# The setup and the first batch of a DFT and bilinear layer kernel in another order: folds as rows arrive, a third table buffer, weight conversion spread over three units

## The chip, the cores and the metric

One core of a Trainium2 chip runs the whole program. TensorE (PE) multiplies, VectorE (DVE), ScalarE (ACT) and GpSimd (POOL) do element work, SyncE (SP) starts most transfers; ACT and POOL start some too. The metric is the device time of one execution in microseconds (us); the median of several runs stands for a kernel.

## The reference

```python
def _attn_ref(x):                      # x: 8 x 3072 x 256, f32
    X = np.fft.fft(x, axis=1)
    X = np.fft.fft(X, axis=2)
    return X.real.astype(np.float32)

def _moe_ref(x, w_a, w_b, w_out):      # 256 x 1536, 256 x 1536, 1536 x 256
    a = x @ w_a
    b = x @ w_b
    return (a * b @ w_out).astype(np.float32)
```

The real part of a two-dimensional DFT over sequence and features is followed by a bilinear layer: two products with weights, multiplied element by element, and a third product. The weights come as 64-bit values and are turned into 32-bit floats on the chip.

## The kernel before

The work is split into high and low halves of each f32 number (`gh` and `gl`, `XH[0]` and `XH[1]`, `W[:, 0]` and `W[:, 1]`), and three products of halves make one f32 product (`PASSES`). The feature DFT is put into the weights: a **weight chunk** (`WChunk`, six of them) multiplies a converted piece of `w_a` or `w_b` by a cosine or sine table `wt` and writes a high and a low half of `W`, and its first row to `w128` by way of DRAM. `Conv` turns a raw 64-bit piece into f32 halves in seven steps: two on ACT ("p", L324 and L325), three on DVE ("a", L326 to L328), the high half on ACT ("b", L329) and the low half on DVE or POOL ("c", L330).

Along the sequence, symmetry folds four row sets to one: `fold_ops` makes for each of three row pairs sums and differences into `F` in twelve operations (numbered 0 to 11 in the code), the even ones on one engine, the odd ones on another. For batch 0 both are DVE; for later batches they are POOL and DVE. `FN` holds the middle column. `xh_split` splits `F` into `XH`, and the chunks **P**, **N0** (or **NA**) and **Q** (`DftP`, `DftN0`, `DftNA`, `DftQ`, 18 matmuls of some 384 columns each) multiply it by tables `tab` that POOL loads into two rotating buffers. Their results are `PQ` (cosine and sine part, two halves each) and `PN` (the Nyquist column). `half` 0 and 1 give the two halves of the sequence.

The loop has 36 **units** per batch, for three column groups `st` and twelve feature tiles `ft`. Unit u does the even matmuls (`mm_e`, L549, six of 512 columns) and the Nyquist term (L553, DVE, which needs `w128`); the down products of the unit before last (`mm_d`, L625, 24 of 256 columns); the odd matmuls (`mm_o`, L564), and for the unit before `post1` (L573 on DVE, a copy `bc` on ACT) and `post2` (the product `g` of L583 on DVE, the mirrored one of L588 on POOL in the first 17 units of batch 0 and on DVE later, the high casts L584 and L589 on ACT, the low halves L592 on POOL). A PSUM pair `ab` is free again after L583. There are two such pairs and four tiles `d`.

Nothing is reordered by a scheduler: the order of the program is the order on each engine (`manual_schedule`). Batch 0 has no batch before it, so its folds, its DFT and the first weight conversions are done in a setup, written out line by line, in a pool `set_p` whose memory `PQ` and `PN` take later. The other conversions, the DFT of `half` 1 and the folds of batch 1 are hung between the units of batch 0 as hooks:

```python
    FOLDS0 = ("raw", (0, 1, 2, 3, 4, 5), (6, 7, 8, 9, 10, 11))
...
    FIRST = {
        0: [DftP(0, 1)],
        1: [DftN0(1)],
        2: [DftQ(0, 1)],
        4: [(conv_in, "a1")],
        5: [(conv_out, "a1")],
...
        13: [(conv_out, "b2"), (nyq.load,)],
        14: [wc[3]],
```

`conv_in` does steps "p" and "a" at one place, `conv_out` "b" and "c" a unit later. `nyq.load` starts 32 transfers of 768 single elements on SP, for the Nyquist columns of the later batches (`NyqTurn`). Partial sums of batch 0 go to DRAM (`part`) and come back.

Of the kernel before, what the change touches and what calls it, by code (L numbers as in the profile page):

```python
# [14 lines left out]
TW = 386  # L15

@with_exitstack
def fft2_real__then__bilinear_moe_kernel(
# [87 lines left out]
    def fold_ops(b, rp, raw, e0, e1, tmp=None):  # L106
# [4 lines left out]
        s1, s2, ms = ((FT if tmp is None else tmp)[:, k] for k in range(3))  # L111
# [163 lines left out]
    class DftQ:  # L275
# [3 lines left out]
        def mm(self):  # L279
# [10 lines left out]
        def post(self, lo_eng=nc.gpsimd):  # L290
            b, half, ps = self.b, self.half, self.ps
            cols, _, _ = halves(half)
            a = bc_p.tile([P, 512], F32, tag="bc", name="bc")
# [58 lines left out]
    class WChunk:  # L352
# [17 lines left out]
        def post(self):  # L370
# [8 lines left out]
            nc.sync.dma_start(w128[:, 4 * c : 4 * c + 4], row)

    def run(fs):
        for f in fs:
            f()
# [639 lines left out]
```

## Time and profile before

| | before |
|---|---|
| median of 3 runs | 1899.04 us (1896.61 to 1900.35) |
| the profiled execution, device time | 1900.28 us |
| its span in the trace | 1898.5 us |
| PE busy | 1790.8 us, 94% |
| DVE, POOL, ACT busy | 1364.7, 1090.4, 698.0 us |
| mean granted PE clock | 0.976 |

The span runs from the first to the last instruction in the trace; 1.8 us of the execution's time lie outside of it. Idle time of an engine counts only where the engine that ends last waits for it. A granted clock of 1.00 is 2.4 GHz and 0.50 is 1.2 GHz.

### The profile page before, as it was taken

The numbers are of one execution on the slowest core, as the hardware profiler recorded it, in microseconds if no ns is written. First come the engines' busy times: TensorE is split into PE (matmuls) and PEld (weight loads), VectorE is DVE, ScalarE is ACT, GpSimd is POOL, SyncE is SP. The second block draws the span as 40 slices with busy tenths as digits, with TensorE's granted clock in tenths as the row PEclk, the third lists the DMA queues.
The fourth block names the chain that finished last, engine by engine and source line by source line (L and its number), as shares of the span: only waits on it lengthen the run. The fifth ranks groups of instructions, "written<-read, shape, count | busy, mean of one in ns | idle before, by whom it ended". The sixth has DMA issues, their size and how long they took to land.

```text
span 1898.5 us, 29035 instructions
## 1 busy us (share of the span) xinstructions
PE 1790.8 (94%) x11146; PEld 1612.0 (85%) x11146; DVE 1364.7 (72%) x2056; ACT 698.0 (37%) x1239; POOL 1090.4 (57%) x887
## 2 busy tenths in 40 slices
PE   2777768999999999999999999999999999999998
PEld 2666657889899998999999989999899998999888
DVE  5556467677876787778776787678776887666766
ACT  2444312433344333333344333333344333333332
POOL 1355455666656665566656665576655666554343
PEclk8798888999999999999999999999999999999999
DMA  6322321332013210222013211222012310210030
GB/s 219 122 93 89 37 78 45 140 98 76 12 57 103 98 45 32 76 89 94 14 56 103 98 45 31 76 90 81 26 57 88 114 45 26 82 56 8 18 26 23
DMA packets 101259, 131.34 MB, mean 69 GB/s; under 512 B 55247, under 2 KB 79967, under 8 KB 94207
## 3 DMA queue, kind: packets, MB, share of 16 engines
q1 hardware_dynamic: 89662, 58.92, 11.0%
q0 software_dynamic: 10896, 70.03, 10.8%
q8 instruction: 87, 1.43, 0.3%
q10 hardware_dynamic: 560, 0.52, 0.1%
q14 instruction: 54, 0.43, 0.1%
HBM read 100.98 MB, written 28.46 MB: 68 GB/s over the span
## 4 chain that ended last, share of the span: by engine, by line
PE 83%; DVE 0%; POOL 0%; ACT 0%; issue 0%; ACTq 0%
PE d L625 39%; PE ab L564 19%; PE ab L549 19%; PE ab L175 5%; PE ab L698 0%; PE ab L694 0%; DVE F L128 0%; POOL gl L592 0%; PE ab L726 0%; PE ab L723 0%; DVE T L573 0%; ACT stg L636 0%; ACTq L528 0%; POOL RAW L118 0%; DVE T L553 0%
## 5 line engine op out<-in xcount | busy, mean ns | idle before, releaser
L592 POOL TENSOR_TENSOR gl<-g,gh 128x512 fp32r<-128x512 f32 x574 | 753.9, 1335 | 595.8 <-ACT gh L584 595.6
L625 PE MATMUL d<-WO,gh 128*128 128x256 f32 x4608 | 830.5, 281 | 0.0
L625 PEld LDWEIGHTS d<-WO,gh 128*128 128x128 f32 x4608 | 728.7, 189 | 26.1 <-ACT stg L636 0.3
L625 PE MATMUL d<-WO,gl 128*128 128x256 f32 x2304 | 647.3, 281 | 0.2
L573 DVE SCALAR_TENSOR_TENSOR T<-T,ab 128x512 f32<-128x512 f32 x576 | 391.5, 685 | 332.5 <-PE ab L564 328.3
L564 PE MATMUL ab<-PQ,W 128*128 128x512 f32 x1728 | 458.6, 401 | 44.1 <-DVE T L553 44.0
L549 PE MATMUL ab<-PQ,W 128*128 128x512 f32 x1728 | 457.6, 400 | 21.2 <-DVE g L583 16.7
L553 DVE SCALAR_TENSOR_TENSOR T<-PN,w,ab 128x512 f32<-128x512 f32 x576 | 412.9, 745 | 78.0 <-PE ab L549 54.6
L625 PEld LDWEIGHTS d<-WO,gl 128*128 128x128 f32 x2304 | 435.6, 189 | 1.5 <-POOL gl L592 1.3
L549 PEld LDWEIGHTS ab<-PQ,W 128*128 128x128 f32 x1728 | 329.3, 191 | 101.4 <-DVE g L583 18.0
L564 PEld LDWEIGHTS ab<-PQ,W 128*128 128x128 f32 x1728 | 307.0, 190 | 101.6 <-DVE T L553 47.5
L574 ACT COPY bc<-ab 128x512 f32<-128x512 f32 x288 | 169.4, 588 | 603.8 <-DVE T L573 603.8
L584 ACT CAST gh<-g 128x512 fp32r<-128x512 f32 x288 | 179.1, 622 | 419.4 <-DVE g L583 416.0
L583 DVE TENSOR_TENSOR g<-ab,bc 128x512 f32<-128x512 f32 x288 | 196.6, 683 | 33.6 <-ACT bc L574 28.9
L588 DVE TENSOR_TENSOR g<-T 128x512 f32<-128x512 f32 x271 | 205.3, 757 | 0.1
L589 ACT CAST gh<-g 128x512 fp32r<-128x512 f32 x288 | 178.7, 621 | 29.7 <-DVE g L588 18.2
L175 PE MATMUL ab<-tab,XH 128*128 128x384 f32 (+1 forms) x576 | 110.3, 346 | 23.9 <-DMA tab<-in_tabs_dram 23.9
L175 PEld LDWEIGHTS ab<-tab,XH 128*128 128x128 f32 x576 | 106.1, 196 | 26.8 <-issue 23.9
L88 POOL TENSOR_TENSOR PQ<-T,PQ 128x768 fp32r<-128x768 f32 x30 | 55.8, 1861 | 37.3 <-ACT PQ L87 29.8
L168 POOL DMA_DIRECT2D tab<-in_tabs_dram x48 | 26.9, 562 | 85.9 <-PE ab L175 85.9
L88 POOL TENSOR_TENSOR XH<-F,XH 128x768 fp32r<-128x768 f32 x30 | 55.7, 1869 | 5.7 <-ACT XH L87 5.7
L636 ACT COPY stg<-d 128x512 f32<-128x512 f32 x94 | 48.2, 596 | 9.2 <-PE d L625 8.1
(138 smaller groups left out, 677.7 us busy)
## 6 DMA issues: line engine op xcount, KB each, us to landing
tab<-in_tabs_dram POOLq DMA_DIRECT2D x48, 1158.0 KB, 5.5
RAW<-in_x_dram SPq DMA_DIRECT2D x44, 256.0 KB
out_dram<-stg SPq DMA_DIRECT2D x36, 256.0 KB
out_dram<-stg SPq DMA_DIRECT2D x12, 512.0 KB
PN<-nrow SPq DMA_DIRECT2D x14, 384.0 KB
out_dram<-stg SPq DMA_DIRECT2D x30, 128.0 KB
RAW<-in_moe_w_out_dram SPq DMA_DIRECT2D x3, 1024.0 KB
part<-stg SPq DMA_DIRECT2D x3, 1024.0 KB
```

The costliest lines, as they stand in the source:

```text
L175: nc.tensor.matmul(ps, lhs(lh, kt), tab[:, kt, rh, 0:n], start=(k == 0), stop=(k == 8))
L549: nc.tensor.matmul(ab[i], W[:, lh, 0, c : c + P], PQ[:, rh, st * 512 : (st + 1) * 512], start=(k == 0), stop=(k == 2), skip_group_check=True,)
L553: nc.vector.scalar_tensor_tensor(t[:, i, :], PN[:, st * 512 : (st + 1) * 512], w128[:, i * NFT + ft : i * NFT + ft + 1], ab[i], ALU.mult, ...
L564: nc.tensor.matmul(ab[i], W[:, lh, 1, c : c + P], PQ[:, 2 + rh, st * 512 : (st + 1) * 512], start=False, stop=(k == 2), skip_group_check=True,
L573: nc.vector.scalar_tensor_tensor(t[:, i, :], t[:, i, :], 2.0, ab[i], ALU.mult, ALU.subtract)
L574: nc.scalar.copy(bc, ab[1])
L583: nc.vector.tensor_tensor(g[:, 0, :], ab[0], bc, ALU.mult)
L584: nc.scalar.copy(gh[:, 0, :], g[:, 0, :])
L588: (nc.gpsimd if v["early"] else nc.vector).tensor_tensor(g[:, 1, ::-1], t[:, 0, :], t[:, 1, :], ALU.mult)
L589: nc.scalar.copy(gh[:, 1, :], g[:, 1, :])
L592: eng.tensor_tensor(gl[:, s, :], g[:, s, :], f32(gh[:, s, :]), ALU.subtract)
L625: nc.tensor.matmul(d[:, s, :], (gh, gl)[lh][:, s, q * P : (q + 1) * P], WO[:, rh, ft, :], start=(ft == first and s == 0 and k == 0), stop= ...
```

## The change

The setup: the row of zeros and its product are made first; each pair of rows is folded wholly when it has come, sums and differences, with the second pair's sums in a conversion's buffers; the middle column `FN` goes from DVE to POOL. A third table buffer `tab2` in the setup's pool holds the table of Q. P, N0 and the second weight chunk write to the `d` tiles of PSUM, so P, N0, Q and the first chunk follow each other. The `post` of each chunk is cut into pieces (`copy`, `sums`, `low`, `high`) that are placed one by one. Weight loads start on ACT's queue, the raw pieces lie in `STG` and `RAWW`, and the last of the setup's conversions is moved into units 0 and 1.

Batch 0: a conversion is spread over three units, its first ACT step a unit ahead of the second and of DVE's; ACT's steps stand between the two high casts of `post2` (`slot`), DVE's behind L583 (now L637). Two of the raw pieces use the table buffers. The 32 gathers are started four per unit over eight units. The folds of batch 1 take three or four operations per unit in units 15 to 26 instead of six in every third unit, and in all later batches the differences go into the buffers of the sums. The Nyquist turn moves from unit 18 to 24.

```diff
@@ fold_ops
-        md1, md2 = xb[:, :, 0:P], xc[:, :, 0:P]
+        md1, md2 = (v[:, :, 0:P] for v in ((xb, xc) if b == 0 else (s1, s2)))
...
-                nc.vector.tensor_tensor(FN[:, q, r2], s1[:, :, P], s2[:, :, P], op)
+                nc.gpsimd.tensor_tensor(FN[:, q, r2], s1[:, :, P], s2[:, :, P], op)
@@ the setup
-        wraw = as_raw(set_p.tile([P, 2048], F32, name="wraw"))
-        FT1 = set_p.tile([P, 3, 2, D], F32, name="FT1")
+        tab2 = set_p.tile([P, 3, 2, TW], F32R, name="tab2")
...
-        cva, cvb, cvo = Conv(wraw, *ca), Conv(STG, *cb), Conv(RAWW, us[0], wo_dst(0))
+        cva, cvb, cvo = Conv(STG, *ca), Conv(RAWW, *cb), Conv(STG, us[0], wo_dst(0))
...
+        rows_zero()
...
-        fold(0, (0, 1, 4, 5))
+        fold(0, (0, 2, 1, 3, 4, 5, 6, 7))
         fold(1, (0, 1, 4, 5))
-        fold(0, (8, 10))
+        wload(STG, wa_src(0), 2, nc.scalar)
+        fold(0, (8, 10, 9, 11))
+        fold(1, (2, 3, 6, 7))
         fold(2, (0, 1, 4, 5))
+        wload(RAWW, wa_src(3), 2, nc.scalar)
+        nc.gpsimd.dma_start(wt.rearrange("p a b c d -> p (a b c d)"), wtab)
+        nc.gpsimd.dma_start(tab2.rearrange("p a b c -> p (a b c)"), tabs[2])
+        tabq[(0, 2)] = tab2
         fold(1, (8, 10))
         fold(2, (8, 10))
+        nc.scalar.copy(XH[:, 0, 0], F[:, 0])
+        fold(1, (9, 11))
+        fold(2, (2, 3))
         fn_split(0)
+        V.tensor_tensor(XH[:, 1, 0], F[:, 0], f32(XH[:, 0, 0]), ALU.subtract)
+        p0.mm(d_tiles(0, 2))
+        n0.mm(d_tiles(1, 3))
+        cva.do("p", V)
+        fold(2, (6, 7, 9, 11))
+        cva.do("a", V)
+        sign_ops(1)
...
+        q0.mm()
+        p0.copy()
+        fn_split(1)
+        cvb.do("p", V)
+        cva.do("c", V)
+        wa0.mm()
...
-    p0.post(V)
-    cva.do("c", V)
-    wa0.mm()
-    cvb.do("p", V)
-    n0.post()
-    q0.mm()
+    p0.sums()
+    n0.copy()
     cvb.do("a", V)
+    p0.extra()
+    q0.copy()
     cvb.do("b", V)
-    wload(STG, wa_src(1), 2)
+    wload(RAWW, wa_src(1), 2)
+    n0.sums()
     cvb.do("c", V)
-    wa0.post()
-    wb0.mm()
-    q0.post(V)
+    wb0.mm(d_tiles(0, 2))
+    wa0.high()
+    p0.low(V)
+    q0.sums()
+    wa0.low()
+    q0.split(V)
+    wb0.high()
     cvo.do("p", V)
+    wb0.low()
     sign_ops(3)
     xh_split(1, 0, nc.gpsimd)
     xh_split(1, 1, nc.gpsimd)
-    wb0.post()
-    cvo.do("a", V)
-    wload(RAWW, wa_src(4), 2)
-    cvo.do("b", V)
-    cvo.do("c", V)
@@ post2 and the units
             if v["early"]:
                 minus()
+                for f, *a in slot:
+                    f(*a)
                 lo(nc.gpsimd, 0)
...
+            minus_high()
             lo(nc.gpsimd, 1)
...
-    FOLDS0 = ("raw", (0, 1, 2, 3, 4, 5), (6, 7, 8, 9, 10, 11))
+    FOLDS0 = ((0, 1, 2), (3, 4, 5), (6, 7, "raw"), (8, 9, 10, 11))
...
+        0: [(cvo.do, "a", V), (cvo.do, "b", V), DftP(0, 1)],
+        1: [(cvo.do, "c", V), (conv_step, 0, "p"), DftN0(1)],
+        2: [DftQ(0, 1), (weights_later,), (conv_step, 0, "a")],
+        16: [(conv_step, 5, "c"), (fold_zero,), (load_part, 0)],
+        24: [(lambda: (nyq.mm(), nyq.post()),), (load_tab, 0, 0), (load_tab, 0, 1)],
...
+    for k in range(1, 6):
+        SLOT[2 * k + 2] = [(conv_step, k - 1, "b"), (conv_step, k, "p1")]
+        SLOT[2 * k + 3] = [(conv_step, k, "p2"), (conv_step, k, "a")]
+        FIRST[2 * k + 3] = [(conv_step, k - 1, "c")]
+    SLOT[15] = [(conv_step, 5, "b")]
+    for k in range(8):
+        FIRST.setdefault(14 + k, []).extend(([(nyq.load,)] if k == 0 else []) + [(nyq.load_rows, k)])
...
-                hook(fold_step, b + 1, i - 18 if b == 0 else i)
+                hook(fold_step, b + 1, i - 15 if b == 0 else i)
```

On ACT, at the end of the setup, before (`ab_189` and `ab_209` are the results of P and N0, `ab_281` that of the first chunk, `ab_302` that of Q):

```order
L214 ACTIVATE bc<-ab_189,zb 128x385
L87 CAST EX<-bc 128x1
L87 CAST PQ<-T 128x768
L324 ACTIVATE u<-stg 128x1024
L325 ACTIVATE s<-stg 128x1024
L240 ACTIVATE bc<-ab_209,zb 128x385
L243 COPY EXN<-bc 1x1
L329 CAST gh<-u 128x1024
L375 CAST W<-ab_281 128x512
```

and now (`d_206` and `d_226` are P and N0, `ab_261` is Q, `ab_292` the first chunk):

```order
L219 ACTIVATE bc<-d_206,zb 128x385
L87 CAST FNH<-FN 128x6
L365 ACTIVATE u<-RAW 128x1024
L366 ACTIVATE s<-RAW 128x1024
L225 CAST PQ<-T 128x768
L262 ACTIVATE bc<-d_226,zb 128x385
L87 CAST EX<-bc 128x1
L323 COPY bc<-ab_261 128x384
L325 COPY EXT<-ab_262 128x1
L370 CAST gh<-u 128x1024
L273 COPY EXN<-bc 1x1
L416 CAST W<-ab_292 128x512
```

The second conversion's two steps now stand ahead of the first cast to `PQ`, and the copies of N0 and Q behind it.

On ACT again, in the units of batch 0, around a conversion, before (`ab_693` and `ab_755` belong to two units that follow each other):

```order
L329 CAST XH<-F 128x1024
L574 COPY bc<-ab_693 128x512
L584 CAST gh<-g 128x512
L589 CAST gh<-g 128x512
L324 ACTIVATE F<-RAW 128x1024
L325 ACTIVATE F<-RAW 128x1024
L574 COPY bc<-ab_755 128x512
```

and now:

```order
L628 COPY bc<-ab_584 128x512
L638 CAST gh<-g 128x512
L370 CAST XH<-F 128x1024
L365 ACTIVATE F<-tabw 128x1024
L645 CAST gh<-g 128x512
L628 COPY bc<-ab_637 128x512
L638 CAST gh<-g 128x512
L366 ACTIVATE F<-tabw 128x1024
L645 CAST gh<-g 128x512
```

The two steps stood together behind both casts to `gh`; now each stands between the two casts of a unit, in two units.

On SP, late in batch 0, before (L379 stores and reads `w128`, L752 are the gathers, L95 row loads of batch 1):

```order
L639 DMA part_384<-stg 128x2048
L748 DMA nyx<-in_mirror_dram 128x128
L752 DMA nyx<-in_x_dram 128x6x1 x32
L379 DMA w_83<-FT 128x1x4
L95 DMA RAW<-in_x_dram 128x512 x2
```

and now:

```order
L807 DMA tabw<-in_mirror_dram 128x128
L813 DMA tabw<-in_x_dram 128x6x1 x4
L418 DMA w_83<-FT 128x1x4
L813 DMA tabw<-in_x_dram 128x6x1 x4
L708 DMA part<-part_374 128x2048
L813 DMA tabw<-in_x_dram 128x6x1 x8
L95 DMA RAW<-in_x_dram 128x512 x2
L813 DMA tabw<-in_x_dram 128x6x1 x12
```

Four gathers stand ahead of the last transfer to `w128` instead of 32; the others lie among the row loads and stores.

## Rows read from the trace of the kernel before

**Rows 1.** Stages: window, its length, then busy us (instructions) of each engine, granted clock.
```profile
0.00:23.87 23.87, 0.00 (x0) 0.00 (x0) 13.16 (x37) 3.58 (x10) 8.36 (x14) 1.00 0.94 343
23.87:79.07 55.20, 31.31 (x116) 26.99 (x117) 30.49 (x48) 23.50 (x36) 7.57 (x7) 0.72 0.34 122
79.07:236.00 156.93, 123.99 (x681) 107.99 (x681) 87.06 (x117) 63.76 (x96) 82.01 (x63) 0.88 0.30 75
236.00:324.00 88.00, 66.43 (x376) 57.28 (x375) 59.53 (x89) 18.89 (x37) 50.04 (x44) 0.88 0.20 66
324.00:1898.50 1574.50, 1569.02 (x9979) 1419.77 (x9977) 1174.46 (x1768) 588.33 (x1060) 942.42 (x760) 1.00 0.20 63
```

**Rows 2.** Waits of PE, 0 to 79.07 us: total, times, longest.
```profile
PE ab L175 <- DMA tab<-in_tabs_dram: 23.9, 1, 23.9
PE ab L364 <- ACT bc L214: 9.5, 1, 9.5
```

**Rows 3.** Waits of PE, 79.07 to 324 us.
```profile
PE ab L564 <- DVE T L553: 37.1, 9, 11.1
PE ab L549 <- DVE g L583: 16.7, 3, 6.8
```

**Rows 4.** Stages again: first of seven half-clock stretches after 79.07 us, their sum.
```profile
128.25:135.08 6.83, 4.85 (x16) 4.29 (x17) 3.78 (x6) 4.53 (x7) 4.58 (x4) 0.50 0.46 155
...
sum 58.03, PE 33.13 PEld 28.08 DVE 31.10 ACT 19.57 POOL 25.91; mean PE 4.73 PEld 4.01 DVE 4.44 ACT 2.80 POOL 3.70
```

**Rows 5.** Chain that ended last, in order of time: start, us, what.
```profile
325.43 1.39 PE ab L564 x6
...
331.04 1.41 PE ab L564 x6
```

**Rows 6.** Timeline (start, us, [idle before]) of first folds; then the stage they open.
```profile
7.98 0.69 DVE L135 TENSOR_TENSOR FT<-RAW 128x512 f32<-128x512 f32 x1 [7.06 <-DMA RAW<-in_x_dram,rix]
...
10.70 0.69 DVE L136 TENSOR_TENSOR FT<-RAW 128x512 f32<-128x512 f32 x1 [2.03 <-DMA RAW<-in_x_dram,rix]
...
7.98:22.77 14.79, 0.00 (x0) 0.00 (x0) 11.97 (x34) 2.29 (x9) 3.02 (x4) 1.00 1.05 407
```

**Rows 7.** Stage of the setup's ACT list; timeline of POOL behind it.
```profile
42.75:63.20 20.45, 12.87 (x45) 10.29 (x45) 11.76 (x17) 13.66 (x23) 1.74 (x3) 0.75 0.45 167
...
62.52 3.58 POOL L88 TENSOR_TENSOR XH<-F,XH 128x768 fp32r<-128x768 f32 x2 [5.69 <-ACT XH L87]
```

**Rows 8.** Timeline around one conversion in the loop.
```profile
121.81 2.54 POOL L592 TENSOR_TENSOR gl<-g,gh 128x512 fp32r<-128x512 f32 x2
...
123.58 1.31 DVE L326 TENSOR_SCALAR F<-F 128x1024 uint32<-128x1024 uint32 x1 [4.25 <-ACT F L324]
125.03 1.23 DVE L327 CUSTOM_DVE_ANT_0 F<-F 128x2048 uint16<-128x2048 uint16 x1
...
130.23 2.93 PE L549 MATMUL ab<-PQ,W 128*128 128x512 f32 x6 [6.79 <-DVE g L583]
```

**Rows 9.** Line L326 in the setup: ns least/median/most, first and last start.
```profile
L326 DVE TENSOR_SCALAR u<-u x2: 686/686/687, 38.6 to 48.7; 128x1024 uint32<-128x1024 uint32 x2
```

**Rows 10.** Groups of DVE, 325 to 337 us: busy us, mean ns.
```profile
L553 DVE SCALAR_TENSOR_TENSOR T<-PN,w,ab 128x512 f32<-128x512 f32 x4 | 2.8, 744 | 0.0
L573 DVE SCALAR_TENSOR_TENSOR T<-T,ab 128x512 f32<-128x512 f32 x4 | 2.6, 682 | 1.4 <-PE ab L564 1.4
...
L583 DVE TENSOR_TENSOR g<-ab,bc 128x512 f32<-128x512 f32 x2 | 1.4, 682 | 0.0
```

**Rows 11.** Timelines of SP's queue and of DVE behind it.
```profile
199.59 22.56 SPq L752 DMA_DIRECT2D nyx<-in_x_dram  x32
...
224.91 0.75 DVE L553 SCALAR_TENSOR_TENSOR T<-PN,w,ab 128x512 f32<-128x512 f32 x1 [11.86 <-DMA w<-FT]
```

**Rows 12.** Timeline of DVE: the Nyquist turn, a fold of batch 1.
```profile
240.41 0.25 DVE L764 TENSOR_TENSOR nyx<-nyx,ab 128x96 f32<-128x96 f32 x1 [2.44 <-PE ab L757]
...
250.24 1.65 DVE L138 TENSOR_TENSOR RAW<-RAW 128x512 f32<-128x512 f32 x1
```

More of the change, by code (lines that the diff above doesn't have):

```diff
@@ L110, in fold_ops @@
         xa, xb, xc, xd = (raw[:, k] for k in range(4))
-        s1, s2, ms = ((FT if tmp is None else tmp)[:, k] for k in range(3))
+        s1, s2, ms = tmp or [FT[:, k] for k in range(3)]
         rv = (slice(None), slice(None, None, -1), slice(None))
@@ L182, in ab_tiles, with d_tiles, dft_pair @@
         return [ps_ab.tile([P, 512], F32, tag=f"ab{i}", name=f"ab{i}") for i in range(2)]
-    def dft_pair(even, odd, half, q, n0):
-        ps = ab_tiles()
+    def d_tiles(*q):
+        return [ps_d.tile([P, 2, D], F32, tag=f"d{k}", name=f"d{k}").rearrange("p a b -> p (a b)") for k in q]
+    def dft_pair(even, odd, half, q, n0, ps=None):
+        ps = ps or ab_tiles()
         m = even(0, 0).shape[-1]
@@ L303, in post, with split @@
             nc.vector.tensor_tensor(t[:, J : J + n1], cv, av[:, ::-1], ALU.subtract)
-            nc.scalar.copy(t[0:1, 0 : 2 * J], PN[0:1, cols])
-            split(lo_eng, PQ[:, 2, cols], PQ[:, 3, cols], t[:, 0 : 2 * J])
+        def split(self, lo_eng=nc.gpsimd):
+            cols, _, _ = halves(self.half)
+            nc.scalar.copy(self.t[0:1, :], PN[0:1, cols])
+            split(lo_eng, PQ[:, 2, cols], PQ[:, 3, cols], self.t)
+        def post(self):
+            self.copy()
+            self.sums()
+            self.split()
     class Conv:
@@ L376, in post, with low @@
             nc.scalar.copy(row.rearrange("o (p f) -> o f p", f=4), ps[1][0:1, :].rearrange("o (f p) -> o f p", f=4))
+            nc.sync.dma_start(w128[:, 4 * c : 4 * c + 4], row)
+        def low(self):
+            c, ps = self.c, self.ps
+            cols = slice(c * 512, (c + 1) * 512)
             for eo in range(2):
                 nc.vector.tensor_tensor(W[:, 1, eo, cols], ps[eo], f32(W[:, 0, eo, cols]), ALU.subtract)
[L379 to L383, printed above, removed]
+        def post(self):
+            self.high()
+            self.low()
     def conv_tiles():
@@ L819, in conv_out, with weights_later @@
-    def conv_out(k):
-        cv[k][0].do("b", V)
-        cv[k][0].do("c", nc.gpsimd)
+    later = [(RAWW, None, us[0], cx)]
+    cv = [Conv(RAWW, us[0], cx)]
+    def weights_later():
+        t = [
+            as_raw(tb_p.tile([P, 3, 2, TW], F32R, tag="tab", name="tabw").rearrange("p a b c -> p (a b c)")[:, 0:2048])
+            for _ in range(2)
+        ]
+        later.extend([
+            (t[0], (wa_src(4), 2), us[1], wo_dst(2)),
+            (t[1], (wo_src(1), 4), us[0], wo_dst(1)),
+            (RAWW, (wa_src(2), 2), us[1], cx),
+            (t[0], (wa_src(5), 2), us[0], wo_dst(2)),
+            (t[1], (wo_src(2), 4), us[1], wo_dst(2)),
+        ])
+        cv.extend(Conv(raw, u, hl) for raw, _, u, hl in later[1:])
+        conv_load(1)
+        conv_load(2)
+        nyq.t = t[0].bitcast(F32).rearrange("p n w -> p (n w)")
@@ L823, in fft2_real__then__bilinear_moe_kernel, with conv_load, conv_step @@
+    def conv_load(k):
+        wload(later[k][0], *later[k][1])
+    def conv_step(k, part):
+        cv[k].do(part, nc.gpsimd)
+        if part == "a" and k < 3:
+            conv_load(k + 3)
     wc = [WChunk(1, wt, *cx), WChunk(4, wt, *wo_dst(2)), WChunk(2, wt, *cx), WChunk(5, wt, *wo_dst(2))]
     FIRST = {
-        0: [DftP(0, 1)],
-        1: [DftN0(1)],
-        2: [DftQ(0, 1)],
-        4: [(conv_in, "a1")],
-        5: [(conv_out, "a1")],
-        6: [(conv_in, "b1"), wc[0]],
-        7: [(conv_out, "b1")],
@@ L934, in fft2_real__then__bilinear_moe_kernel @@
                     late_post = None
+                if prev is None or not prev["early"]:
+                    for f, *a in u[5]:
+                        f(*a)
                 if len(pend) >= 2:
```

164 lines of the change are left out of this document (79 added, 85 removed).

## The prediction

> **What bounds the kernel now.** I read the stage table first [rows 1]. From 324 us on TensorE is busy 1569.02 of 1574.50 us at a granted clock of 1.00; nothing in this change can shorten that. All that is to be had lies in the first 324 us. There PE is busy 31.31 + 123.99 + 66.43 = 221.7 us, so it is idle 102.3 us, and its clock is 0.72, 0.88 and 0.88 in the three working stages. The waits of PE say what for. Up to 79.07 us it is the start (23.9 us, a table of the DFT) and the setup (9.5 us, an ACT copy ahead of the first weight matmul) [rows 2]. From there to 324 us it is DVE: 37.1 us for the Nyquist term of L553 (longest 11.1) and 16.7 us for the product of L583 that frees a PSUM pair [rows 3]. No DMA stands in those two rows, but one is behind the longest wait, as the SP queue below shows.
>
> The lost clock is a cost of the same waits. In seven stretches at 0.50 (1.2 of 2.4 GHz), 58.03 us long, PE was busy 33.13 us [rows 4]; at 2.4 GHz that work takes half, so 16.6 us were lost, 2.4 per stretch. Each opens in or right behind an idle time of PE: the one from 128.25 [rows 4] in the wait of 6.79 us that ends at 130.23 [rows 8]. So the 244.9 us from 79.07 to 324 hold 190.4 us of PE work, which is 190.4 - 16.6 = 173.8 at the full clock, 54.5 of idleness and 16.6 of clock.
>
> A unit that nothing holds up takes PE 331.04 - 325.43 = 5.61 us, 1.39 of it the six odd matmuls [rows 5]. In the stage from 79.07 to 236 us DVE is busy 87.06 and POOL 82.01 us [rows 1], PE 123.99, some 113 of it at full clock. So in the units with weight conversion no other engine is the bound on average; order and latency are. From 236 to 324 us DVE has 59.53 us and PE, at full clock, about 60: there DVE has no room.
>
> **The change part by part.** *The setup, until the second unit begins (79.07 before).* The differences of rows 1 and half of those of rows 2 now stand on DVE ahead of the low half of XH, and the six small FN sums leave it. DVE needed 11.97 us from its first fold at 7.98 to the end of that half [rows 6]; four more operations of 512 columns (0.69 each [rows 6]) and four of half that width, less the small sums, make about 3.5. The second pair of rows came at 10.70 [rows 6]; DVE does two operations before it needs them, which leaves a hole of about 1.5. So XH is whole at 7.98 + 11.97 + 3.5 + 1.5 = 24.9, where the table let PE begin at 23.87. The weight loads no longer compete with the table, but DVE is then the limit: no gain at the start, a loss of 1 at most. The gain comes behind it: with the zero rows, FNH and a table for Q all there, P, N0 and Q run without the 9.5 us stop. A 512-column matmul takes 1.39/6 = 0.232 us, one of 384 columns 0.174 by proportion, 18 of them 3.1; the first group at half clock 6.3: 24.9 + 6.3 + 3.1 + 3.1 = 37.4. The first weight chunk follows at once.
>
> The new wait: PQ lies in memory that the third table buffer had, so ACT's first PQ cast waits for Q to end, at 37.4, and 20 more ACT instructions stand behind it, up to the sign flips and the XH casts that the second P needs. Before, the same kind of list, 42.75 to 63.20, held 13.66 us of ACT work [rows 7]; it loses a bias copy and one two-step preparation and gains two W casts and a row copy, so I take 13.0. ACT ends at 50.4, POOL's low half (3.58/2 = 1.8 [rows 7]) at 52.2, and the second P, 18 matmuls at half clock, at 58.5; the first unit fits in beside the casts. **The second unit begins at 58.5 instead of 79.07: -20.6 us.** Bounds: -12 (rows late, ACT held by DVE) to -24.
>
> *Conversions in the loop.* Before, the two ACT steps stood behind both gh casts, and all three DVE steps waited for them, in front of L573. Around 125 us that reads: L326 at 123.58, L327 at 125.03, L328 after it, and PE waits until 130.23, 6.79 us [rows 8]. Now the first ACT step stands a unit earlier and DVE finds its input. In such a unit DVE does 2 x 0.682 + 2 x 0.744 + 0.682 = 3.53 us of L573, L553 and L583 [rows 10], then 0.69 [rows 9] + 1.23 [rows 8] + 1.23 for L328 of the same width, to 6.68, then the next L573 and L553, 2.85, to 9.53. PE comes to the odd matmuls that need these at 5.61 + 5.61 - 1.39 = 9.83; since each half of a PSUM pair is released by itself, another 0.7 is slack: 1.0 in all.
>
> But POOL runs now while DVE converts. L326 shows that price: 0.686 us in the setup [rows 9], 1.31 when it began under a POOL pair that ran from 121.81 to 124.35 [rows 8]; it ended 0.54 us after POOL did, so it stood still meanwhile. L327 and L328 always met an idle POOL, so their price under one is not shown. A POOL operation takes 1.27 us (2.54/2 [rows 8]) and there are three in a unit. Bounds: nothing, or three of them less the slack, 3.8 - 1.0 = 2.8 us for each of six conversions, 17 us. I take 1.3 us, nearly two of them, 8 us in all, since L326 met one each time that POOL was at work. The ACT steps that now stand ahead of the second gh cast are in it.
>
> The Trainium skill, SBUF — State Buffer, section "SBUF: two separate sides", says that GpSimd and a DVE operation with two SBUF inputs or in a two-port mode take one shared port pair by an exclusive lock, the loser standing still for the whole instruction. The trace agrees for L326 (1.31 us, above). By that rule L327 and L328 pay as L326 does; it speaks against a change that first puts them under POOL work, and the sum by it is the first rival below.
>
> *The SP queue.* 32 gathers of single elements took 22.56 us of SP, with the 2 KB of w128 behind them, for which DVE waited 11.86 us [rows 11]. Now four gathers (2.8 us) stand ahead of that store, and a unit lies between it and its reader: nothing is left of the 11.1 us of PE idleness. The other gathers share SP with the row loads of batch 1.
>
> *Folds of batch 1.* Three operations per unit in units 15 to 26, not six in every third. The differences go into the sum buffers, so RAW is free one step earlier and a load has two units (11.2 us) to land, not one. Rows 2 of batch 1 still stand behind six stores and four gathers; I leave 2 us there, and 3 us for DVE under POOL: L138 took 1.65 us at 250.24 [rows 12], where an operation of 512 columns alone takes 0.69 [rows 6]. Units 15 and 16 carry a POOL product, a conversion's low half and folds: 2 us. The Nyquist turn, now at unit 24, makes DVE wait 2.44 us [rows 12] as before, but in a unit with folds: 2.5 us. Units 1 to 3, with the end of the setup's conversions: 1 us.
>
> **Sum of the loop.** 173.8 + 8 + 5 + 2 + 2.5 + 1 = 192.3, and 2.4 for one stretch at half clock: 194.7 instead of 244.9, **-50.2 us**. From batch 1 on nothing: PE is full there [rows 1], and the new homes of the differences only lengthen the time that rows may take. Together 20.6 + 50.2 = 70.8. The profiled execution took 1900.28 us (span 1898.5 and 1.8 around it), 1.2 above the median of the three runs: 1900.3 - 70.8 = 1829.5, say **1830 us**.
>
> **The rivals.** *DVE under POOL becomes the bound.* Every DVE step of a conversion stands still for one POOL operation: 17 us instead of 8; two half-clock stretches more, 4.8; 5 more in the folds, where DVE has no room: 1830 + 9 + 4.8 + 5 = 1849. For it speaks the 1.65 us of L138; against it, that no row shows L327 under POOL. It is the rule of the Trainium skill named above, worked out from rows.
>
> *The setup gains half.* ACT's list waits for DVE at each step, and Q ends later because its table lands late: the second unit begins at 69, 1840 us. The ACT copy in rows 2 speaks for it; that the weight operands are ready ahead of PE speaks against it.
>
> *Nothing stands any more.* Conversions and folds hide wholly: 8 + 5 + 2 + 2.4 less, and 24 for the setup: 1809 to 1813.
>
> *Slower.* The gathers hold up batch 1: 28 of 32 now stand among loads that POOL and DVE need. If each of the three groups of rows waits for a whole former queue of 22.56 us and loses one stretch of clock, 75 us go again: 1905. It decides from 70.8/3 = 23.6 us per group on. Against it: at most eight gathers (5.6 us) stand between the row loads' turn and their issue, with two units of lead.
>
> **How the numbers follow.** Forecast 0.52, DVE under POOL 0.21, half the setup 0.13, nothing left 0.10, level or slower by the gathers 0.04. The range takes in the first three and the upper edge of the fourth: 1812 to 1851. A measurement here tells 0.2% (4 us) from no change; every case but the last is faster: 0.96, 0.02 within, 0.02 slower.
>
> **What will show it.** Right: PE without a wait between P and the first weight chunk; ACT's first PQ cast right after Q; the second unit near 58 us; DVE's wait for w128 gone; PE full from about 255 us. Wrong: the first P before 22 or after 27 us; the conversion's steps on DVE stretched to 2 us or more each; PE waits of 4 us at the folds; row loads that land after their fold's turn.

## The result, and the profile after

The changed kernel takes 1829.06 us (median of 4; the kernel before, beside it, 1899.69): a ratio of 0.9632, 95% interval 0.9616 to 0.9649. The forecast was 1830. Its profiled span is 1827.2 us, 71.3 less than before. One execution of e9 (3539.3 us) took about twice and one of e2 (9950.5 us) over five times as long as the others of the run, and the ratios below leave them out.

The stages, as in [rows 1]: window, length, busy us (instructions) of PE, PEld, DVE, ACT and POOL, granted clock. The second unit begins at 56.36; the last stage is as long as before's from 324 on, 1574.5 us, and holds the same PE work, so the stage ahead of it is the old 79.07 to 324.

```profile
0.00:21.88 21.88, 1.87 (x9) 1.81 (x9) 15.58 (x39) 3.47 (x9) 12.70 (x18) 1.00 0.87 322
21.88:56.36 34.48, 28.24 (x109) 23.29 (x109) 28.99 (x39) 22.00 (x35) 8.54 (x9) 0.90 0.54 197
56.36:252.70 196.34, 180.22 (x1060) 157.28 (x1061) 152.26 (x207) 83.82 (x138) 140.19 (x108) 0.97 0.35 95
252.70:1827.20 1574.50, 1568.94 (x9972) 1419.93 (x9970) 1184.66 (x1766) 586.74 (x1059) 942.15 (x760) 1.00 0.20 63
...
151.26:154.68 3.42, 3.42 (x17) 3.22 (x16) 2.36 (x4) 2.86 (x5) 3.42 (x4) 0.50 0.00 0
226.36:233.18 6.82, 5.55 (x13) 4.33 (x14) 4.91 (x11) 2.21 (x6) 3.27 (x5) 0.50 0.16 34
```

So the part up to the second unit is 79.07 - 56.36 = 22.7 us shorter (forecast 20.6), and the loop behind it 244.9 - 196.34 = 48.6 (forecast 50.2). In the loop two stretches at half clock are left of seven [rows 4]; they cost (3.42 + 5.55) / 2 = 4.5 us instead of 16.6.

PE's waits, as in [rows 2, 3]: 0 to 56.36, then 56.36 to 145, then 145 to 252.7. The 2.3 of the second unit's start is counted in the first and the second group.

```profile
PE d L176 <- DMA tab<-in_tabs_dram: 16.0, 1, 16.0
...
PE ab L603 <- DVE g L637: 2.3, 1, 2.3
PE ab L618 <- DVE T L607: 1.9, 1, 1.9
PE d L176 <- DVE XH L515: 0.8, 1, 0.8
...
PE ab L603 <- DVE g L637: 5.8, 4, 2.3
PE d L685 <- POOL gl L648: 2.4, 4, 0.8
PE ab L618 <- DVE T L607: 2.3, 2, 1.1
...
PE ab L618 <- DVE T L607: 4.6, 3, 3.4
PE ab L603 <- DVE g L637: 2.5, 1, 2.5
```

The stop of 9.5 us for L214 and the 11.1 us behind `w128` are gone, and behind the table's arrival no wait is longer than 3.4 us.

### The profile page after: what moved, and what is told of

It is laid out like the page before. It is cut to its first block, busy times and chain, and to the rows that moved or that the text cites. A ratio compares the mean times of both kernels' runs of the same rounds, so it can differ in the third digit from the quotient of the medians.

```text
span 1827.2 us, 29055 instructions
## 1 busy us (share of the span) xinstructions
PE 1779.3 (97%) x11146; PEld 1602.3 (88%) x11146; DVE 1381.5 (76%) x2050; ACT 696.0 (38%) x1239; POOL 1103.6 (60%) x893
## 3 DMA queue, kind: packets, MB, share of 16 engines
q0 software_dynamic: 10896, 70.03, 11.2%
## 4 chain that ended last, share of the span: by engine, by line
PE 91%; DVE 3%; POOL 2%; issue 1%; DMA 1%; ACT 1%; SPq 1%; ACTq 0%; DVEq 0%; POOLq 0%
PE d L685 42%; PE ab L618 21%; PE ab L603 21%; PE ab L176 6%; POOL gl L648 1%; SPq L813 0%; DVE T L627 0%; POOL g L642 0%; PE ab L405 0%; PE d L176 0%; DVE T L607 0%; DMA RAW<-in_x_dram,rix 0%; DMA w<-FT 0%; DVE F L368 0%; DVE F L367 0%
## 5 line engine op out<-in xcount | busy, mean ns | idle before, releaser
L648 POOL TENSOR_TENSOR gl<-g,gh 128x512 fp32r<-128x512 f32 x574 | 760.6, 1346 | 573.5 <-ACT gh L638 569.3
L618 PE MATMUL ab<-PQ,W 128*128 128x512 f32 x1728 | 454.9, 399 | 8.9 <-DVE T L607 8.8
L603 PE MATMUL ab<-PQ,W 128*128 128x512 f32 x1728 | 452.1, 396 | 9.7 <-DVE g L637 8.3
L607 DVE SCALAR_TENSOR_TENSOR T<-PN,w,ab 128x512 f32<-128x512 f32 x576 | 412.9, 745 | 58.0 <-PE ab L603 44.1
L603 PEld LDWEIGHTS ab<-PQ,W 128*128 128x128 f32 x1728 | 324.7, 189 | 89.6 <-DVE g L637 10.4
L618 PEld LDWEIGHTS ab<-PQ,W 128*128 128x128 f32 x1728 | 305.1, 189 | 65.2 <-DVE T L607 11.2
L637 DVE TENSOR_TENSOR g<-ab,bc 128x512 f32<-128x512 f32 x288 | 196.8, 683 | 40.3 <-ACT bc L628 31.9
L176 PE MATMUL ab<-tab,XH 128*128 128x384 f32 (+1 forms) x558 | 104.7, 341 | 0.1
L176 PEld LDWEIGHTS ab<-tab,XH 128*128 128x128 f32 x558 | 100.3, 191 | 3.3 <-POOL XH L88 0.6
L100 POOL DMA_INDIRECT RAW<-in_x_dram,rix x44 | 44.3, 1008 | 10.6 <-issue 8.7
```

What stands on the lines that cost most here:

```text
L176: nc.tensor.matmul(ps, lhs(lh, kt), tab[:, kt, rh, 0:n], start=(k == 0), stop=(k == 8))
L603: nc.tensor.matmul(ab[i], W[:, lh, 0, c : c + P], PQ[:, rh, st * 512 : (st + 1) * 512], start=(k == 0), stop=(k == 2), skip_group_check=True,)
L607: nc.vector.scalar_tensor_tensor(t[:, i, :], PN[:, st * 512 : (st + 1) * 512], w128[:, i * NFT + ft : i * NFT + ft + 1], ab[i], ALU.mult, ...
L618: nc.tensor.matmul(ab[i], W[:, lh, 1, c : c + P], PQ[:, 2 + rh, st * 512 : (st + 1) * 512], start=False, stop=(k == 2), skip_group_check=True,
L637: nc.vector.tensor_tensor(g[:, 0, :], ab[0], bc, ALU.mult)
L648: eng.tensor_tensor(gl[:, s, :], g[:, s, :], f32(gh[:, s, :]), ALU.subtract)
```

## The experiments

A run's loop is its span less 1574.5 us and less the start of its second unit (196.3 in the changed kernel). The start and the setup vary by themselves, so the loop tells more than the median of a few runs. It is read from one execution of each run; the changed kernel's two give 196.3 and 196.2.

| run | median us | ratio to before, 95% | second unit | loop |
|---|---|---|---|---|
| e1_rows_later | 1825.8 | 0.9619 (0.9607 to 0.9631) | 56.6 | 193.8 |
| e2_gathers_behind | 1826.8 | 0.9628 (0.9615 to 0.9640) | 57.2 | 193.2 |
| e3_xh_on_dve | 1830.6 | 0.9648 (0.9634 to 0.9661) | 58.8 | 195.5 |
| e4_act_together | 1827.7 | 0.9632 (0.9619 to 0.9644) | 57.6 | 197.5 |
| e5_gathers_at_once | 1835.5 | 0.9674 (0.9654 to 0.9694) | 58.1 | 201.3 |
| e6_no_third_table | 1834.9 | 0.9669 (0.9651 to 0.9686) | 62.8 | 197.5 |
| e7_folds_in_lumps | 1832.5 | 0.9658 (0.9640 to 0.9675) | 55.5 | 200.9 |
| e9_slot_behind | 1830.5 | 0.9654 (0.9636 to 0.9671) | 56.2 | 196.8 |
| e10_slot_behind_together | 1828.6 | 0.9645 (0.9630 to 0.9660) | 56.4 | 194.9 |
| e11_three_moves | 1820.7 | 0.9601 (0.9588 to 0.9614) | 57.7 | 189.2 |
| e12_changed_again | 1829.6 | 0.9643 (0.9630 to 0.9656) | 58.5 | 196.2 |

### The setup: the third table, and POOL beside DVE

```diff
-            if half == 1:
-                load_tab(half, 2)
+            load_tab(half, 2)
...
-        nc.gpsimd.dma_start(tab2.rearrange("p a b c -> p (a b c)"), tabs[2])
-        tabq[(0, 2)] = tab2
```

> The changed kernel, with the table of Q loaded into the two rotating buffers again, when P and N0 have read them; the memory of the third buffer stays reserved, so that nothing else moves. Theory of the prediction (the third table lets Q follow N0 at once, and the first weight chunk after it): Q waits for a load that can only start when N0 ends at 32.0 and takes some 4 to 6 us, so Q, the first chunk, and ACT's first cast to PQ behind it come 4 to 6 us later, and a stretch of clock is lost with it: 1833 to 1838. Rival: ACT's list sets the second unit, not Q, and has slack against TensorE: 1829 to 1831.

PE's timeline from N0 on (start, us, [idle before]):

```profile
29.27 3.35 PE L176 MATMUL d<-tab,FNH 128*128 128x386 f32 x18
37.02 6.01 PE L176 MATMUL ab<-tab,XH 128*128 128x384 f32 x18 [4.41 <-DMA tab<-in_tabs_dram]
```

Q waits 4.41 us and then takes 6.01, at a granted clock of 0.50 from 35.98 to 42.80; the changed kernel's Q takes 3.34 from 31.86. The second unit comes 6.4 us later and the time is 5.8 higher: the theory holds. The second unit of the other ten runs begins between 55.5 and 58.8, so the third table is worth some 4 to 7 of the setup's 22.7 us.

```diff
-    xh_split(1, 0, nc.gpsimd)
-    xh_split(1, 1, nc.gpsimd)
+    xh_split(1, 0, V)
+    xh_split(1, 1, V)
```

> The changed kernel, with the two low halves of XH for the second P on DVE instead of POOL. Theory: while POOL makes them (4.61 us from 48.07) DVE's two conversion steps stand still: L368 took 2.77 and L369 2.74 us, against 1.23 each alone. On DVE the two halves take about 0.9 us each, L368 and L369 fall back to 1.23, so DVE is done 3.1 - 1.8 = 1.3 us sooner, and the wait of 2.29 us ahead of the second unit falls to about 1: time 1827 to 1828. Rival: L368 and L369 are slow for what they read and write there, not for POOL: they keep 2.7 us, DVE is 1.8 us later, time 1831.

DVE and POOL in the changed kernel:

```profile
48.21 2.77 DVE L368 CUSTOM_DVE_ANT_0 F<-F,FT 128x2048 uint16<-128x2048 uint16 x1
51.02 2.74 DVE L369 SCALAR_TENSOR_TENSOR F<-stg,F 128x1024 uint32<-128x1024 uint32 x1
...
48.07 4.61 POOL L88 TENSOR_TENSOR XH<-F,XH 128x768 fp32r<-128x768 f32 x2 [12.05 <-DVE F L367]
```

and DVE in the experiment:

```profile
49.98 1.83 DVE L88 TENSOR_TENSOR XH<-F,XH 128x768 fp32r<-128x768 f32 x2 [2.62 <-ACT XH L87]
51.73 1.40 DVE L607 SCALAR_TENSOR_TENSOR T<-PN,w,ab 128x512 f32<-128x512 f32 x2
...
53.77 1.22 DVE L368 CUSTOM_DVE_ANT_0 F<-F,FT 128x2048 uint16<-128x2048 uint16 x1
55.02 1.22 DVE L369 SCALAR_TENSOR_TENSOR F<-stg,F 128x1024 uint32<-128x1024 uint32 x1
```

With POOL idle both steps take 1.22 us: the stall is POOL's. No time was won, which the theory had missed: in program order the two halves now stand ahead of L607, and wait 2.62 us there for ACT.

### The conversions

```diff
-        SLOT[2 * k + 2] = [(conv_step, k - 1, "b"), (conv_step, k, "p1")]
-        SLOT[2 * k + 3] = [(conv_step, k, "p2"), (conv_step, k, "a")]
+        SLOT[2 * k + 2] = [(conv_step, k - 1, "b")]
+        SLOT[2 * k + 3] = [(conv_step, k, "p"), (conv_step, k, "a")]
```

> The changed kernel, with the first ACT step of each of five conversions moved back to the unit of the second: both stand between the two casts to gh in front of DVE's steps, so the spread over three units is two again. Theory of the prediction (the step a unit ahead lets DVE find its input): DVE starts each conversion 1.1 us later, and the second cast to gh comes 1.1 us later too; the slack is 1.0, so each conversion costs 0.5 to 1.5 us more and the five some 3 to 8 us: time 1832 to 1837, with waits for L607 and L637 at each. Rival: what costs in a conversion is DVE under POOL alone; ACT has room (it is busy 48.11 us of 93.64 in this stretch), and the time stays within 1829 plus or minus 1.5.

Nothing that can be measured in the time: the loop is 1.2 us longer, the median 1.4 lower. Next, the slot behind both casts, alone and with the edit above:

```diff
                 minus()
-                for f, *a in slot:
-                    f(*a)
                 lo(nc.gpsimd, 0)
...
             minus_high()
+            for f, *a in slot if v["early"] else ():
+                f(*a)
             lo(nc.gpsimd, 1)
```

> The changed kernel, with the conversion's steps back behind both casts to gh (the second of which waits for POOL's product), the first ACT step still a unit ahead. Since moving that first step changed nothing, this asks whether the place between the casts is what made conversions cheap. Theory: it is: the second ACT step and DVE's three start 1 to 3 us later than now, with a slack of 1.0, so five conversions cost 3 to 10 us more: 1832 to 1839. Rival: either of the two moves is enough by itself, since one ACT step of 1.1 us is what fits into the slack: 1829 to 1831.

> The changed kernel, with both ACT steps of a conversion together and behind both casts to gh, as in the kernel before. Theory: this is the old order, so waits of the old size return: DVE starts 3 to 4 us later than now and each of five conversions costs 2 to 5 us, half clock behind some: 1840 to 1855. If the two moves each suffice alone, this one alone of the three runs is slow. Rival: the old waits came from elsewhere (raw pieces that arrive late in one buffer, w128), and this stays under 1834.

By the time both rivals were right: loops of 196.8 and 194.9 us. By the waits they were not. In e10, with ACT's order that of before, PE waits for L607 behind the conversions of units 5, 9 and 11:

```profile
98.68 2.79 PE L618 MATMUL ab<-PQ,W 128*128 128x512 f32 x6 [2.85 <-DVE T L607]
130.27 1.67 PE L618 MATMUL ab<-PQ,W 128*128 128x512 f32 x6 [0.91 <-DVE T L607]
145.58 2.06 PE L618 MATMUL ab<-PQ,W 128*128 128x512 f32 x6 [3.55 <-DVE T L607]
```

Behind those of units 5 and 11, e4 waits 3.63 and 3.66 us and e9 3.38 and 3.43, and some 3.4 us at a granted clock of 0.50 follow each. The changed kernel does not wait for L607 there, only 0.8 us each time for POOL's `gl`, and 0.4 more a unit later. What is lost there is won back behind unit 12's chunk: the changed kernel waits 2.48 us there (e1, below), and these three do not. Units count from 0, so the second unit is unit 1; from the start of unit 4 (78.88 in the changed kernel) PE takes:

| kernel | us to unit 12's chunk | to unit 13 | to unit 15 |
|---|---|---|---|
| before | 78.13 | 87.25 | 104.12 |
| changed | 65.82 | 71.21 | 87.16 |
| e12_changed_again | 65.71 | 71.11 | 87.07 |
| e4_act_together | 69.22 | 73.15 | 87.60 |
| e9_slot_behind | 69.72 | 73.64 | 88.60 |
| e10_slot_behind_together | 68.43 | 72.41 | 86.64 |

So ACT's order is worth 2.6 to 3.9 of the 12.3 us won up to unit 12's chunk, and the next wait hides most of it. No run takes it back in a kernel without that next wait.

PE's waits in the kernel before, 79.07 to 190 us:

```profile
PE ab L549 <- DVE g L583: 16.7, 3, 6.8
PE ab L564 <- DVE T L553: 5.0, 2, 3.0
```

Before, five of six conversions cost 16.7 + 5.0 = 21.7 us (the last, in unit 15, cost nothing). The three that waited for L583 are those of units 6, 8 and 12, which also hold a weight chunk; the two in units without one (4 and 10) made up the 5.0, 2.97 and 2.06. The change also moved DVE's steps to units 5, 7, 9, 11 and 13, and the chunks stand in 6, 8, 12 and 14. In e10 the conversions of units 5 and 11, with no chunk just ahead, cost about what those of units 4 and 10 cost before, and the three of units 7, 9 and 13, behind a chunk, cost 0.9. So what is left as the main cause is that a conversion and a chunk no longer share a unit. That is argued by exclusion: no run puts them together again. A second candidate is POOL: in unit 6 the low half of the conversion before stood ahead of L588, and ACT's second cast waited 1.89 us for it:

```profile
118.20 2.40 POOL L330 TENSOR_TENSOR XH<-F,XH 128x1024 fp32r<-128x1024 f32 x1 [0.87 <-ACT XH L329]
...
121.89 0.62 ACT L589 CAST gh<-g 128x512 fp32r<-128x512 f32 x1 [1.89 <-POOL g L588]
```

In unit 12 that cast waited 2.89 us for POOL, and PE 6.23. In unit 8 the low half was long done, POOL itself waited for DVE,

```profile
139.13 1.29 POOL L588 TENSOR_TENSOR g<-T 128x512 f32<-128x512 f32 x1 [2.42 <-DVE T L573]
```

and PE still waited 3.65 us. By these rows 3 x 3.65 = 11 of the 16.7 us would be the shared unit's and the rest POOL's, which is an estimate: no run put either back, so how they divide stays open.

### The SP queue

The kernel before, with the gathers behind the last `w128` store:

```diff
-        13: [(conv_out, "b2"), (nyq.load,)],
+        13: [(conv_out, "b2")],
...
-        15: [(conv_in, "o2")],
+        15: [(conv_in, "o2"), (nyq.load,)],
...
-        18: [(lambda: (nyq.mm(), nyq.post()),)],
         19: [(load_part, 0)],
+        20: [(lambda: (nyq.mm(), nyq.post()),)],
```

> The kernel before, with one thing changed: the 32 gathers start in unit 15 instead of 13, behind the last store to w128, and the Nyquist turn is done in unit 20 instead of 18 to leave them their time. Theory: the longest wait of TensorE, 11.1 us for L553 behind w128, goes with its half clock, 11 to 14 us: 1886 to 1889. Rival: the gathers now stand ahead of the row loads of unit 18, whose folds come late by as much: 1895 to 1900.

It took 1887.5 us, 8.5 less than the median of the kernel before in its batch (1896.0); the ratio is 0.9941 (0.9920 to 0.9962), which is 7 to 15 us. PE's waits from 79 to 324 us, against 37.1 in [rows 3]:

```profile
PE ab L564 <- DVE T L553: 25.9, 8, 9.5
```

11.2 us of waiting went. The opposite, in the changed kernel:

```diff
-        FIRST.setdefault(14 + k, []).extend(
+        FIRST.setdefault(14, []).extend(
```

> The changed kernel, with all 32 gathers of the Nyquist columns started in unit 14, ahead of the last store to w128, as the kernel before had them in unit 13. Theory (order on SP): the store of 2 KB stands behind 22 to 25 us of gathers, L607 waits for it about 8 to 12 us as L553 did before (11.86), a stretch of half clock follows (2.4): 1839 to 1844, less the 6 us that the last row loads gain since no gather stands ahead of them any more: 1833 to 1838. Rival: a store of 2 KB on SP is not held by gathers ahead of it (its wait before was for the chunk itself), then no wait for w128 and about 1823.

SP's queue, and DVE behind it, as in [rows 11]:

```profile
159.85 23.71 SPq L813 DMA_DIRECT2D tabw<-in_x_dram  x32
...
185.87 0.75 DVE L607 SCALAR_TENSOR_TENSOR T<-PN,w,ab 128x512 f32<-128x512 f32 x1 [10.46 <-DMA w<-FT]
```

The old wait is back, 10.46 us. The order on SP is the cause, from both sides.

### What is left in the loop: rows and folds

```diff
-        if b == 1 and i == -4:
+        if b == 1 and i == -3:
```

> The changed kernel, with the first row loads of batch 1 issued one unit later (12, not 11). Theory: the 2.48 us wait of TensorE at 147.61 us, and the half clock behind it (3.41 us long, 1.7 lost), come from POOL, which issues two indirect row loads (1.05 and 0.98 us, from 144.46) right behind a conversion's low half of 2.40 us and so makes its product of L642 late. One unit later POOL has a chunk's 2.9 us more and no low half in front: the wait falls to under 0.7 us and the time by 3 to 4 us, to about 1825. Rival: the wait is that of the chunk's order (its matmuls take both PSUM pairs, so the product of L637 is late whatever POOL does): then the wait stays over 2 us, and the time at 1829.

POOL and PE in the changed kernel (the second load, 0.98 us from 145.82, left out):

```profile
141.91 2.40 POOL L371 TENSOR_TENSOR XH<-F,XH 128x1024 fp32r<-128x1024 f32 x1
144.46 1.05 POOL L100 DMA_INDIRECT RAW<-in_x_dram,rix  x1 [0.15 <-issue]
...
146.81 1.29 POOL L642 TENSOR_TENSOR g<-T 128x512 f32<-128x512 f32 x1
...
150.09 1.97 PE L603 MATMUL ab<-PQ,W 128*128 128x512 f32 x6 [2.48 <-DVE g L637]
```

and PE in the experiment:

```profile
149.86 1.43 PE L603 MATMUL ab<-PQ,W 128*128 128x512 f32 x5 [0.83 <-DVE g L637]
```

The wait falls from 2.48 to 0.83 us, the time by 3.3 and the loop by 2.5: the theory names the right cause. The half clock is not part of it: the repetition of the changed kernel (e12) has the same wait with none behind it:

```profile
152.67 1.66 PE L603 MATMUL ab<-PQ,W 128*128 128x512 f32 x6 [2.51 <-DVE g L637]
```

```diff
-        FIRST.setdefault(14 + k, []).extend(
+        FIRST.setdefault(14 + k + (k == 7), []).extend(
```

> The changed kernel, with the last four gathers of the Nyquist columns one unit later (22, not 21), so that they stand behind the last row loads of batch 1 on SP. Theory: those four took SP 9.22 us from 210.74, the row loads came at 220.05, the folds of L136 and L137 at 223.56 and 224.12, and TensorE waited 3.44 us and ran 6.83 us at half clock: with the rows first that wait is gone, and the time falls by 5 to 7 us, to about 1823. Rival: the rows are late since SP stands in the stores of L582 (207.64 to 210.68) and not in the gathers, or the gathers are then late for the Nyquist turn in unit 24: the wait stays or moves to L818 and the time is 1829 or more.

SP, DVE and PE in the changed kernel:

```profile
210.74 9.22 SPq L813 DMA_DIRECT2D tabw<-in_x_dram  x4
220.05 1.06 SPq L95 DMA_DIRECT2D RAW<-in_x_dram  x2
...
224.12 1.25 DVE L137 TENSOR_TENSOR FT<-RAW 128x512 f32<-128x512 f32 x1 [4.88 <-DMA RAW<-in_x_dram]
...
227.28 2.93 PE L618 MATMUL ab<-PQ,W 128*128 128x512 f32 x6 [3.44 <-DVE T L607]
```

and in the experiment:

```profile
211.96 3.28 SPq L95 DMA_DIRECT2D RAW<-in_x_dram  x2
...
225.59 0.73 PE L618 MATMUL ab<-PQ,W 128*128 128x512 f32 x2 [0.61 <-DVE T L607]
```

The wait falls to 0.61 us and no clock is lost there, so the theory names the right cause; but the loop is only 3.2 us shorter and the median 2.3 lower, where 5 to 7 were expected. A wait of 1.33 us for L607 that ends at 233.62 is new, and takes back a part; one of 1.54 at 162.94 is not the move's, since e12 has it too (at 164.33).

```diff
-    FOLDS0 = ((0, 1, 2), (3, 4, 5), (6, 7, "raw"), (8, 9, 10, 11))
+    FOLDS0 = ((), (0, 1, 2, 3, 4, 5), (6, 7, "raw", 8, 9, 10, 11), ())
```

> The changed kernel, with the folds of batch 1 in lumps of six in two of four units, where the row loads stay at their units. Theory: three more operations on DVE in a unit, 0.7 to 1.25 us each, on 4.2 us of its other work make 6.3 to 8 us against TensorE's 5.6 and a slack of 1.0: 0 to 1.4 us of waiting per lump, six lumps, and POOL's operations delay gl: 3 to 8 us more, 1832 to 1837. Rival: DVE and POOL make it up in the empty units between, since two pairs of PSUM buffers stand between them and TensorE: 1829 plus or minus 1.5.

The loop is 4.5 us longer and the time 3.4 higher: spreading is worth about that.

### A faster version

The first two moves together, and the two low halves of XH on DVE, around L368:

```diff
-    xh_split(1, 0, nc.gpsimd)
-    xh_split(1, 1, nc.gpsimd)
+    nc.scalar.copy(XH[:, 0, 0], F[:, 2])
+    nc.scalar.copy(XH[:, 0, 1], F[:, 3])
...
+    def xh_low(q):
+        V.tensor_tensor(XH[:, 1, q], F[:, 2 + q], f32(XH[:, 0, q]), ALU.subtract)
...
-        0: [(cvo.do, "a", V), (cvo.do, "b", V), DftP(0, 1)],
+        0: [(cvo.steps[2], V), (xh_low, 0), (cvo.steps[3], V), (xh_low, 1), (cvo.steps[4], V), (cvo.do, "b", V), DftP(0, 1)],
```

> The changed kernel with the first row loads in unit 12, the last four gathers in unit 22, and the two low halves of XH on DVE, one ahead of and one behind L368, so that DVE never waits for the casts. Theory: the first two give what they gave alone, 3.5 and 3.4 us, since they act in different units; the third takes L368 and L369 from 2.77 and 2.74 back to 1.23 and adds 2 x 0.95, 1.2 us: together 7 to 8 us, 1820 to 1822. Rival: what is won in one unit is given back by the next wait, as one of the gather move's waits was (1.33 us for L607 at 232): 1823 to 1826.

> The changed kernel itself, beside the next three on one chip. Both theories: 1826 to 1831, as before, and the second unit somewhere between 55.5 and 57.3 us, which is how much the start and the setup moved among six runs that share its setup.

1820.7 us against 1829.6 for the changed kernel on the same chip: 8.9 less. That is more than the parts that are known: alone, the first two moves gave 3.3 and 2.3 us by their medians. The third was not run alone, but here the second unit begins 11.1 us after the second chunk's row copy (L417, at 46.56) where it begins 12.7 after it in the changed kernel, so it gives about 1.6. The loop, with no half clock in it:

```profile
57.66:247.00 189.34, 176.42 (x1061) 154.00 (x1062) 150.69 (x207) 83.68 (x138) 142.00 (x109) 1.00 0.37 98
```

## Why the prediction was right, and where it was not

**The start.** The first matmul of P came at 21.88 with the table and the low half of XH at 23.57 (22.62 + 0.95 for L515); forecast 24.9 for the latter. The zero rows, now loaded first, held up nothing, and the first fold began at 6.02 instead of 7.98 [rows 6], which the sum had left as it was. From there DVE took 17.6 us, and the sum had 17.0. The half clock that the sum put down for P is in no row: the granted clock is 1.00 there, in the kernel before too. P was slow all the same, 5.22 us for its last 16 matmuls, where N0's 18 took 3.33. Why stays open.

```profile
21.88:28.85 6.97, 6.20 (x19) 5.69 (x20) 6.43 (x11) 4.48 (x7) 1.60 (x4) 1.00 0.92 329
...
23.63 5.22 PE L176 MATMUL d<-tab,XH 128*128 128x386 f32 x16 [0.77 <-DVE XH L515]
...
33.65 0.84 ACT L225 CAST PQ<-T 128x768 fp32r<-128x768 f32 x1 [1.66 <-PE ab L176]
```

With 1.3 us less for XH and 1.1 less for P, Q ended at 31.86 + 3.34 = 35.2 instead of 37.4.

**The setup's end.** That P, N0, Q and the chunk run without a stop was right, and e6 shows what one stop costs. ACT's first cast to PQ did wait for Q, 1.66 us, but not to its end: it began at 33.65, 1.5 us ahead of it. ACT's list, up to the casts of XH, then ran to 48.72, in 15.1 us instead of 13.0, of which it was busy 12.7. So the second P began at 49.04 instead of 52.2, and at half clock for only a part of its time (mean 0.68) it took 5.03 us instead of 6.3. The step that failed is the last: the second P was to set the second unit, at 58.5. It ended at 54.07; what PE then waited for, 2.29 us, was DVE, whose L368 and L369 took 5.5 instead of 2.45 us under POOL's two halves. Two errors of opposite sign, 4.4 early and 2.3 late, made 56.36: that this was near is partly luck. In the ten other runs with the third table the unit began between 55.5 and 58.8, so the forecast lies at their upper edge.

**Conversions.** The price left over was near: 8 forecast; PE's waits from 56.36 to 145 are 5.8 + 2.4 + 2.3 less the 2.3 of the second unit's start and 1.4 in unit 2 (1 was forecast for units 1 to 3), 6.8 us. But only 2.3 of these are what the sum priced, L607 behind a DVE step that POOL held up, in units 7 and 9; 2.4 are POOL's `gl`, which the sum did not have, and 2.1 stand behind the chunks of units 6 and 8. So the size is partly luck. The reason given for the gain carries the smaller part of it. It was said to lie in ACT's first step a unit ahead and DVE finding its input; e4, e9 and e10 take that away, and of the 12.3 us won up to unit 12's chunk they lose 2.6 to 3.9. What remained the same in all three is that no conversion of units 5 to 13 shares a unit with a weight chunk; the prediction read the 6.79 us from 123.44 as ACT's lateness and did not see that this unit held a chunk.

**DVE under POOL.** Right, and the first rival wrong in degree: each conversion of the loop pays once, not at every step. POOL's low half ran from 105.45 to 107.88, and DVE under it reads:

```profile
106.20 2.23 DVE L367 TENSOR_SCALAR F<-F 128x1024 uint32<-128x1024 uint32 x1
108.57 1.23 DVE L368 CUSTOM_DVE_ANT_0 F<-F,FT 128x2048 uint16<-128x2048 uint16 x1
```

2.23 - 0.69 = 1.54 us are lost, near the 1.3 assumed. L368 stood still only in the setup.

**The SP queue.** Right in cause and size: 11.1 us of PE's idleness were forecast to go. In e8 11.2 went, and in e5 a wait of DVE of 10.46 came back; in the changed kernel's loop DVE never waits for `w128`.

**Folds, units 15 and 16, Nyquist turn.** Forecast 5, 2 and 2.5. Measured 4.6 of waits for L607 from 145 us on, 3.44 of it the last rows, late behind four gathers. They took SP 9.22 us where the slower rival's counterargument allowed eight gathers 5.6; that rival's mechanism was there, once and small. Units 15 and 16 cost nothing, but POOL's row loads at unit 11, two issues of 1 us that were not counted at all, cost 2.48. The turn cost 0.35. Half clock took 4.5 us where 2.4 was put down. PE's own work came to 180.2 - 4.5 = 175.7 us instead of 173.8. The errors nearly cancel, which is luck: 194.7 forecast, 196.3 measured.

**The signs.** Two signs of being wrong came true, a first P before 22 us (21.88) and row loads that land after their fold's turn (DVE waited 4.88 us). A third did in part: each conversion had one DVE step of over 2 us, not all three.

## What to carry to other kernels

When a matmul waits, list everything else in that unit before naming a cause: here a chunk shared the unit with the conversion, and the order on the engine that stood in the row (ACT) was worth 2.6 to 3.9 of 12.3 us. When a run's time does not move, compare its waits too, over the whole stretch: two waits of 3.4 to 3.7 us came back in e4 and e9, and one of 2.48 went. A transfer's start is work for its engine too, on POOL as on SP; put row loads ahead of many small gathers, and not behind an engine's longest operation. A total that comes out right can hide steps that are wrong by several us in both directions.

## What was unexpected of the hardware

DVE and POOL stop each other in both directions. While DVE's L368 kept its 1.23 us, a pair of L648 on POOL took 4.59 instead of 2.55 us, and then L369 took 2.21:

```profile
90.63 1.23 DVE L368 CUSTOM_DVE_ANT_0 F<-F 128x2048 uint16<-128x2048 uint16 x1 [1.09 <-ACT F L366]
91.89 2.21 DVE L369 SCALAR_TENSOR_TENSOR F<-tabw,F 128x1024 uint32<-128x1024 uint32 x1
...
90.66 4.59 POOL L648 TENSOR_TENSOR gl<-g,gh 128x512 fp32r<-128x512 f32 x2
```

The Trainium skill, SBUF — State Buffer, section "SBUF: two separate sides", says that when GpSimd meets a DVE operation with two SBUF inputs or in a two-port mode, whichever starts first has the shared ports for its whole instruction, while the other is fully blocked; this stretch and e3 agree.

Starting four single-element gathers took SP 3.68 us at 158.11 and 9.22 at 210.74; 32 in one go took 23.71, 0.74 each. In e2, where the row loads go first at that place, loads and gathers took 3.28 + 7.14 = 10.42 us, and 9.22 + 1.06 = 10.28 in the changed kernel, so it is the place, behind six stores of L582, that is dear, and not the gathers alone. Why was not tried.

The setup moves by 2 us with one small transfer: the second chunk's row copy waits until the first's store to `w128` has read the row, 0.63 us in the changed kernel's trace and 2.62 in its repetition. In all nine runs that leave this part as it is, the second unit begins 12.7 to 12.8 us after that copy starts:

```profile
45.70 1.04 ACT L417 COPY FT<-d 1x512 f32<-1x512 f32 x1 [2.62 <-DMA w<-FT]
```
